# Image lines from two queues, fewer TensorE instructions ahead of the last one, pooled sums on VectorE: a start-up change to a fused attention and feed-forward kernel

**Chip, cores, metric.** One core of one Trainium2 chip. The metric is device time in microseconds (us), the median of several executions; a profile is one such execution. All times "at" a point are us from the start of the profiled span.

## The reference, cut to what matters

Four images are pooled 4x4, projected, and used as both keys and values of an attention with 12288 queries per image; the 49152 results go through a gated feed-forward layer.

```python
kv_pool = kv.reshape(B, H // r, r, W // r, r, C).mean(axis=(2, 4))      # r = 4, C = 128
k = v = kv_pool.reshape(B, -1, C) @ w_sr                                 # 768 keys per image
a = softmax(q @ k.transpose(0, 2, 1) / sqrt(C))
x = (a @ v).reshape(B * N, C)                                            # 49152 x 128
out = (relu(x @ w_gate) * (x @ w_val)) @ w_out                           # d_ff = 1536
```

## The kernel before

Queries are handled in tiles of 512. A loop over tiles `k` has twelve steps; in each, TensorE does one score, value, feed-forward and output matmul or so, of four different tiles. Before the loop, the first image has to be loaded, pooled, transposed and projected, and the first four tiles need scores. The 768 keys come as three pairs of 128-key chunks; each pair is loaded as four "lines" of 512 KB (rows `dh` of the 4x4 pooling). A "bank" in the code is a piece of the memory that takes TensorE's results; an "accumulator" is a bank that is held while several matmuls add into it. A load "lands" when its last byte has arrived.

```python
def kv_load(b, pair):                       # four loads of 512 KB on SyncE's queue
    ...
    for dh in range(r):
        nc.sync.dma_start(parts[:, dh]..., rows[dh])

def turn_add(chunk, lines, first=False):    # pool by transposing matmuls, summed in a bank
    if first: kv_Ts[chunk] = bank([128, 128])
    for i in range(lines.shape[1]):
        nc.tensor.matmul(kv_Ts[chunk], lines[:, i], ident, is_transpose=True, ...)

def values(k, jc, half):                    # two matmuls of 129 columns
    if jc == 0: x_banks[k, half] = bank([128, 2, C + 1])   # held until the last jc
    ...
# ---- first pair: four lines through TensorE as they land
for dh in range(3):
    for h in range(2): turn_add(h, line(0, dh, h), first=dh == 0)
...  # last line, projection, queries, eight scores
# ---- second pair: lines 0+1 added on VectorE, line 2, the sum and line 3 through TensorE
s1 = add_pixels(add_lines(1)); attend(0, 0)
...
for h in range(2):
    for half in range(2): values(1, h, half)       # first values of tiles 1 and 2
    project_chunk(2 + h, nc.scalar)
scores(0, 2); values(2, 0, 0); scores(0, 3); ...
attend(0, 1)
# ---- weights and the next queries on GpSimd's queue, gated behind line 2 of the third pair
nc.gpsimd.tensor_copy(gate, line(2, 2)[:, 0, 0, 0:1])
...  # wv, wg (halves), queries of group 1
q_turn(1)                                          # a transposing load, SBUF to SBUF: qT
nc.gpsimd.dma_start(wo16, ...)
# ---- last image line, then the loop
```

The transposing load `qT` gives the queries of tiles 4 to 7.

The softmax here doesn't subtract the row's maximum and nothing guards it: scores larger than these inputs give would overflow.

Of the kernel before, what the change touches and what calls it, by code (L numbers as in the profile page):

```python
# [10 lines left out]
FP16 = mybir.dt.float16  # L11
AF = mybir.ActivationFunctionType
ALU = mybir.AluOpType
# [3 lines left out]
def kernel(  # L17
# [23 lines left out]
    nc = tc.nc  # L41
# [5 lines left out]
    NJC = J // 128  # L47
# [7 lines left out]
    GRP = 4  # L55
# [8 lines left out]
    const = ctx.enter_context(tc.tile_pool(name="const", bufs=1))  # L64
# [4 lines left out]
    def bank(shape, dtype=FP32):  # L69
        return psum.tile(shape, dtype, tag="bank", name="bank_ps")  # L70
# [53 lines left out]
    def qT_of(k):  # L124
        s0 = (k % GRP) * NS
        return qTs[k // GRP][:, s0 : s0 + NS, :].rearrange("c s p -> c (s p)")
# [3 lines left out]
    kv16 = const.tile([128, B, NJC, 2 * C + 16], FP16)  # L130
    kv_in = {}

    def kv_load(b, pair):
        parts = work.tile([128, r, 2, r, C], FP32, tag="kv_in", bufs=3)
        rows = kv[b, pair * 2 * HC : (pair + 1) * 2 * HC].rearrange(
            "(hp dh) (wp h dw) c -> dh hp wp (h dw c)", dh=r, h=2, dw=r
        )
        for dh in range(r):
            nc.sync.dma_start(parts[:, dh].rearrange("p h dw c -> p (h dw c)"), rows[dh])  # L139
        kv_in[b, pair] = parts  # L140

    s3s, kv_Ts, key_banks = {}, {}, {}
# [15 lines left out]
    def turn_add(chunk, lines, first=False):  # L158

        if first:  # L160
            kv_Ts[chunk] = bank([128, 128])
        for i in range(lines.shape[1]):
            nc.tensor.matmul(  # L163
                kv_Ts[chunk], lines[:, i], ident, is_transpose=True,
                start=first and i == 0, stop=False, skip_group_check=True,
            )

    def turn_end(chunk, lines, engine=nc.vector):
        turn_add(chunk, lines)
        if chunk % 2 == 0:  # L170
            kv_Ts["pair"] = work.tile([128, 2, 128], FP32, tag="kvT", bufs=2, name="kvT")
        kvT = kv_Ts["pair"][:, chunk % 2]
        if engine is nc.scalar:
            nc.scalar.copy(kvT, kv_Ts[chunk])
        else:
            nc.vector.tensor_copy(kvT, kv_Ts[chunk])
        kv_Ts[chunk] = kvT

    def project_chunk(jc, engine=nc.vector):
        pr = bank([128, 128])  # L180
        nc.tensor.matmul(pr, w_sr_f32, kv_Ts.pop(jc), start=True, stop=True)  # L181
        if engine is nc.scalar:
            nc.scalar.mul(kv16[:, 0, jc, 0:C], pr, 1.0 / (r * r))  # L183
        else:
            nc.vector.tensor_scalar(kv16[:, 0, jc, 0:C], pr, 1.0 / (r * r), None, op0=ALU.mult)
# [9 lines left out]
    def turn_values(b, pair):  # L195
        vt = bank([128, 2, 128], FP16)
        for h in range(2):
            nc.tensor.transpose(vt[:, h], kv16[:, b, 2 * pair + h, 0:C], ident16)
        nc.vector.tensor_copy(kv16[:, b, 2 * pair : 2 * pair + 2, C : 2 * C], vt)
# [26 lines left out]
    def scores(k, jc):  # L226
        if jc == 0:
            aTs[k] = work.tile([128, NJC, T], FP16, tag="aT", bufs=4, name="aT")
        s_ps = bank([128, T])
        nc.tensor.matmul(s_ps, kv16[:, k // NST, jc, 0:C], qT_of(k), start=True, stop=True)  # L230
        nc.scalar.activation(aTs[k][:, jc, :], s_ps, AF.Exp, scale=qk_scale)  # L231

    def values(k, jc, half):
        if jc == 0:
            x_banks[k, half] = bank([128, 2, C + 1])
            if half == 0:
                x16s[k] = work.tile([128, NS, C], FP16, tag="x16", bufs=3, name="x16")
        x_ps = x_banks[k, half]
        for i in range(2):
            s = 2 * half + i  # L240
            nc.tensor.matmul(  # L241
                x_ps[:, i, :], aTs[k][:, jc, s * 128 : (s + 1) * 128],
                kv16[:, k // NST, jc, C : 2 * C + 1],
                start=(jc == 0 and i == 0), stop=(jc == NJC - 1), skip_group_check=True,
            )
# [150 lines left out]
    ident = const.tile([128, 128], FP32)  # L396
    make_identity(nc, ident)
    ident16 = const.tile([128, 128], FP16)
# [1 line left out]
    nc.gpsimd.memset(kv16[:, :, :, 2 * C : 2 * C + 16], 1.0 / X_SCALE)  # L400

    w_sr_f32 = const.tile([128, C], FP32)
    nc.scalar.dma_start(w_sr_f32, w_sr)
    kv_load(0, 0)
    for i in range(0, GRP, 2):
        q_load_plain(i, i + 2)
    for pair in range(1, NJC // 2):
        kv_load(0, pair)

    filler = const.tile([128, 512], FP16)  # L410
    nc.vector.memset(filler, 1.0)
    warm = const.tile([128, 1], FP32)
    nc.vector.memset(warm, 0.0)
    nc.scalar.activation(warm, warm, AF.Exp)
# [6 lines left out]
    idle = bank([128, 512])  # L421

    def fill(n):
        for _ in range(n):
            nc.tensor.matmul(idle, ident16, filler, start=True, stop=True)

    fill(8)

    def attend(k, pair):
        for jc in (2 * pair, 2 * pair + 1):  # L430
            for half in range(2):
                values(k, jc, half)

    def line(pair, dh, h=slice(0, 2)):
        return kv_in[0, pair][:, dh, h]

    def add_lines(pair):
        s2 = work.tile([128, 2, r, C], FP32, tag="kv_s2", bufs=2, name="kv_s2")
        nc.vector.tensor_tensor(s2, line(pair, 0), line(pair, 1), op=ALU.add)
        return s2  # L440

    def add_pixels(s2):
        s1 = work.tile([128, r, C], FP32, tag="kv_s1", bufs=2, name="kv_s1")
        s1 = s1.rearrange("p (h i) c -> p h i c", h=2)
        nc.vector.tensor_tensor(s1, s2[:, :, 0:2], s2[:, :, 2:4], op=ALU.add)
        return s1

    def scores_of(k, pair):
        for jc in (2 * pair, 2 * pair + 1):
            scores(k, jc)  # L450

    for dh in range(3):
        for h in range(2):
            turn_add(h, line(0, dh, h), first=dh == 0)
    for h in range(2):
        turn_end(h, line(0, 3, h), (nc.vector, nc.scalar)[h])
    for h in range(2):
# [11 lines left out]
    scores_of(2, 0)  # L469
    scores_of(3, 0)  # L470

    s1 = add_pixels(add_lines(1))
    attend(0, 0)
    for h in range(2):
        turn_add(2 + h, line(1, 2, h), first=True)
    for h in range(2):
        turn_add(2 + h, s1[:, h])
    for h in range(2):
        turn_end(2 + h, line(1, 3, h), nc.scalar)
    for h in range(2):  # L480
        for half in range(2):
            values(1, h, half)
        project_chunk(2 + h, nc.scalar)
    s2 = add_lines(2)
    scores(0, 2)
    values(2, 0, 0)
    scores(0, 3)
    scores(1, 2)
    scores(1, 3)
    values(2, 1, 0)  # L490
    scores_of(2, 1)
    nc.vector.tensor_tensor(s2[:, 0], s2[:, 0], line(2, 2)[:, 0], op=ALU.add)
    turn_values(0, 1)
    s1 = add_pixels(s2)
    turn_add(5, line(2, 2, 1), first=True)
    attend(0, 1)

    gate = const.tile([128, 1], FP32)
    nc.gpsimd.tensor_copy(gate, line(2, 2)[:, 0, 0, 0:1])
# [6 lines left out]

    for h in range(2):
        turn_add(4 + h, line(2, 3, h), first=h == 0)
    for h in range(2):
        turn_end(4 + h, s1[:, h], (nc.vector, nc.scalar)[h])  # L510
    scores(3, 2)
    for h in range(2):
        for half in range(2):
            values(1, 2 + h, half)
        project_chunk(4 + h, (nc.vector, nc.scalar)[h])
    scores_of(0, 2)
    turn_values(0, 2)
    for jc in (2, 3):
        values(2, jc, 0)
    scores_of(1, 2)  # L520
    attend(0, 2)
    for half in range(2):
        keep_sums(0, half)
# [6 lines left out]
    for jc in range(NJC - 2):  # L530
        values(2, jc, 1)
    late = [(2, 5), (3, 4), (3, 5)]
    left = {2: [(2, jc, half) for half in range(2) for jc in range(NJC - 2, NJC)]}
    for step, k, half in ((4, 3, 0), (7, 3, 1)):
        left[step] = [(k, jc, half) for jc in range(NJC // 2)]
        left[step + 1] = [(k, jc, half) for jc in range(NJC // 2, NJC)]
# [5 lines left out]
    for k in range(LAG, last + 1):  # L542
# [4 lines left out]
        b = k // NST + 1  # L547
        at = k % NST - (NST - NJC - 6)
        for step in range(NFB):
            kO, kF = k - LAG - 1, k - LAG  # L550
            half, i = divmod(step // 2, NJC // 2)
# [47 lines left out]
            if b < B:  # L599
                if step == 1 and 0 <= at < NJC and at % 2 == 0:  # L600
                    kv_load(b, at // 2)
                if step == 3 and 0 <= at - 2 < NJC:
                    pool_pixels(nc.gpsimd, b, (at - 2) // 2, at % 2)
                pair, odd = divmod(at - 4, 2)
                if 0 <= pair < NJC // 2:
                    if not odd and step == 1:
                        moves = turn_blocks(b, pair)
                    if moves and step > 4:
                        nc.sync.dma_start(*moves.pop())
                    if odd and step == 10:  # L610
                        project(b, pair)
                pair, odd = divmod(at - 6, 2)
                if 0 <= pair < NJC // 2 and not odd and step == 1:
                    turn_values_dma(b, pair)
# [33 lines left out]
```

## Time and profile before

| | before |
|---|---|
| median of runs (first five) | 1033.91 us (1033.40 to 1034.15) |
| profiled execution | 1033.09 us, span 1031.3 |
| TensorE busy | 99% |
| last image line lands | 23.09 |
| first instruction fetch of TensorE | 20.95, for 1.09 us |
| first feed-forward matmul ("loop start") | 30.30 |
| first output matmul (second pass) | 38.40 |

From about 34 us on TensorE is never idle for long, so a microsecond won ahead of that can be worth a microsecond at the end. And the profiled execution is one of the fastest of this kernel (1033.09 against a median of 1033.91), so totals of single profiles can't be compared at this scale; the times at which things happen inside them can.

### The profile page before, as it was taken

To read this page: it belongs to the slowest core of one execution; us is meant where nothing else is said; L and a number is where in the kernel's file an instruction comes from. 1 tells how busy PE (TensorE), PEld (TensorE's weight loads), DVE (VectorE), ACT (ScalarE), POOL (GpSimd) and SP (SyncE) were. 2 spreads that over 40 slices of the span, in tenths; PEclk is the share of its full clock that TensorE was granted. 3 is DMA by queue.
4 is the path that set the end of the run, shared out by engine and by line. 5 is a ranking of instruction groups with operands and counts; after the bars stand their busy time and mean duration, and the time that the engine had idled before them with its cause. 6 is when DMAs were issued, how large, how long until landed. Compare 5 with 4: busy or idle time off the path is not lost.

```text
span 1031.3 us, 20032 instructions
## 1 busy us (share of the span) xinstructions
PE 1024.4 (99%) x6580; PEld 546.0 (53%) x6580; DVE 910.0 (88%) x1671; ACT 908.8 (88%) x1745; POOL 279.4 (27%) x287
## 2 busy tenths in 40 slices
PE   8999999999999999999999999999999999999998
PEld 6555555555555555555555555555555555555555
DVE  3889899998989898998889898989888898989898
ACT  4988888889888889888888898888888988888987
POOL 2212146521211125642212121664121221111110
PEclk9999999999999999999999999999999999999999
DMA  8836396462542547836345157573652434513222
GB/s 305 122 57 76 90 195 144 79 93 42 82 69 48 80 120 162 169 53 90 52 68 86 33 84 151 131 173 57 85 73 46 73 54 65 87 32 65 34 40 54
DMA packets 328824, 93.34 MB, mean 91 GB/s; under 512 B 308496, under 2 KB 321936, under 8 KB 328720
## 3 DMA queue, kind: packets, MB, share of 16 engines
q1 hardware_dynamic: 313488, 78.69, 38.7%
q0 software_dynamic: 14944, 13.24, 10.9%
q8 instruction: 51, 0.84, 0.4%
q14 instruction: 53, 0.43, 0.1%
q10 hardware_dynamic: 288, 0.13, 0.0%
HBM read 53.94 MB, written 26.35 MB: 78 GB/s over the span
## 4 chain that ended last, share of the span: by engine, by line
PE 98%; ACT 1%; DMA 1%; SPq 0%; DVE 0%; issue 0%; ACTq 0%
PE bank_ps L279 24%; PE bank_ps L290 24%; PE bank_ps L314 23%; PE bank_ps L241 13%; PE bank_ps L230 12%; PE bank_ps L300 1%; DMA parts<-in_kv_dram 1%; PE bank_ps L163 1%; ACT aT L231 0%; PE bank_ps L189 0%; PE bank_ps L181 0%; SPq L139 0%; ACT val L283 0%; ACT kv L183 0%; PE bank_ps L119 0%
## 5 line engine op out<-in xcount | busy, mean ns | idle before, releaser
L293 DVE SCALAR_TENSOR_TENSOR hT<-bank_ps,val 128x512 f16<-128x512 f32 x1152 | 757.9, 686 | 91.1 <-ACT val L283 70.5
L283 ACT CAST val<-bank_ps 128x512 f16<-128x512 f32 x1152 | 677.8, 589 | 102.5 <-PE bank_ps L279 100.5
L279 PE MATMUL bank_ps<-xT,wv 128*128 128x512 f16 x1152 | 436.6, 379 | 0.2 <-DVE rinv L249 0.2
L290 PE MATMUL bank_ps<-xT,wg 128*128 128x512 f16 x1152 | 436.6, 379 | 0.0
L314 PE MATMUL bank_ps<-hT,wo 128*128 128x512 f16 x1116 | 423.0, 379 | 0.0
L231 ACT ACTIVATE aT<-bank_ps 128x512 f16<-128x512 f32 x576 | 345.8, 604 | 1.0 <-PE bank_ps L230 1.0
L324 POOL TENSOR_SCALAR o_sb<-o_t 128x512 f32<-128x512 f32 x93 | 138.3, 1487 | 694.1 <-DVE rinv L249 660.0
L241 PEld LDWEIGHTS <-aT 128*128 128x128 f16 x2304 | 177.3, 98 | 133.1 <-issue 0.9
L241 PE MATMUL bank_ps<-kv,aT 128*128 128x129 f16 x2304 | 223.6, 220 | 0.0
L230 PE MATMUL bank_ps<-qT,kv 128*128 128x512 f16 x576 | 217.3, 379 | 0.4 <-DVE qT L122 0.2
L279 PEld LDWEIGHTS <-wv 128*128 128x128 f16 x1152 | 112.7, 98 | 132.7 <-issue 0.3
L290 PEld LDWEIGHTS <-wg 128*128 128x128 f16 x1152 | 112.7, 98 | 67.3
L314 PEld LDWEIGHTS <-wo 128*128 128x128 f16 x1116 | 109.2, 98 | 65.9 <-issue 0.2
L230 PEld LDWEIGHTS <-kv 128*128 128x128 f16 x576 | 56.1, 98 | 67.6 <-issue 0.8
L257 DVE TENSOR_TENSOR x<-bank_ps,rinv 128x256 f16<-128x256 f32 x190 | 80.6, 424 | 6.6
L322 DVE STREAM_TRANSPOSE o_t<-bank_ps 128x512 f32<-128x512 f32 x93 | 65.7, 706 | 0.0
L86 POOL DMA_DIRECT2D q<-in_q_dram x88 | 48.3, 556 | 0.3 <-issue 0.3
L148 POOL TENSOR_TENSOR s<-parts 128x512 f32<-128x512 f32 x36 | 44.8, 1265 | 0.0
L249 DVE RECIPROCAL rinv<-bank_ps 128x2 f32<-128x2 f32 x192 | 27.9, 146 | 0.8 <-PE bank_ps L241 0.8
L150 POOL TENSOR_TENSOR s<-s 128x512 f32<-128x512 f32 x18 | 22.8, 1266 | 1.4
L152 POOL TENSOR_TENSOR c<-s 128x256 f32<-128x256 f32 x18 | 13.0, 724 | 1.4
L300 PEld LDWEIGHTS <-hT 128*128 128x128 f16 x144 | 10.1, 98 | 5.8
(53 smaller groups left out, 94.6 us busy)
## 6 DMA issues: line engine op xcount, KB each, us to landing
parts<-in_kv_dram SPq DMA_DIRECT2D x48, 512.0 KB, 6.5
out_dram<-o_sb SPq DMA_DIRECT2D x353, 64.0 KB, 2.2
q<-in_q_dram POOLq DMA_DIRECT2D x88, 128.0 KB, 4.6
xT<-x SPq DMA_TRANSPOSE x94, 2.4
out_dram<-o_sb SPq DMA_DIRECT2D x80, 16.0 KB, 1.5
placed<-blocks SPq DMA_DIRECT2D x9, 128.0 KB, 1.8
kvT<-placed SPq DMA_DIRECT2D x36, 32.0 KB, 1.9
q<-in_q_dram SPq DMA_DIRECT2D x2, 512.0 KB, 8.0
```

The costliest lines, as they stand in the source:

```text
L86: nc.gpsimd.dma_start(q16[32 * j : 32 * (j + 1)].rearrange("t (i s) c -> t i s c", i=GRP), rows[j])
L230: nc.tensor.matmul(s_ps, kv16[:, k // NST, jc, 0:C], qT_of(k), start=True, stop=True)
L231: nc.scalar.activation(aTs[k][:, jc, :], s_ps, AF.Exp, scale=qk_scale)
L241: nc.tensor.matmul(x_ps[:, i, :], aTs[k][:, jc, s * 128 : (s + 1) * 128], kv16[:, k // NST, jc, C : 2 * C + 1], start=(jc == 0 and i == 0) ...
L257: nc.vector.tensor_tensor(x16s[k][:, 2 * half : 2 * half + 2, :], x_ps[:, :, 0:C], rinv.to_broadcast([128, 2, C]), op=ALU.mult,)
L279: nc.tensor.matmul(va_ps, wv16[:, fb * 128 : (fb + 1) * 128], xTs[k], start=True, stop=True)
L283: nc.scalar.copy(val, va_ps)
L290: nc.tensor.matmul(g_ps, wg16[:, fb * 128 : (fb + 1) * 128], xTs[k], start=True, stop=True)
L293: nc.vector.scalar_tensor_tensor(hTs[k][:, fb, :], g_ps, 0.0, vals.pop((k, fb)), op0=ALU.max, op1=ALU.mult)
L314: nc.tensor.matmul(o_banks[k], wo16[:, fb, :], hTs[k][:, fb, :], start=fb == 0, stop=fb == NFB - 1)
L322: nc.vector.transpose(o_t, o_banks.pop(k))
L324: nc.gpsimd.tensor_scalar(o_sb.rearrange("t j s c -> t s j c"), o_t.rearrange("t (s j c) -> t s j c", s=NS, j=4), 1.0 / X_SCALE**2, None, ...
```

## The change

Intent: load the first four lines from two issuing engines; keep TensorE's instruction count ahead of the last image line low enough that the fetch of its next instructions doesn't share the DMA engines with that line; for that, add lines on VectorE and move twelve first value matmuls behind the line. (The prediction and the text below speak of "the title's 192": the title under which the change was handed over named that figure for the instruction count.)

```diff
-    def kv_load(b, pair):
+    def kv_load(b, pair, queues=(nc.sync,)):
...
-            nc.sync.dma_start(parts[:, dh]..., rows[dh])
+            queues[dh % len(queues)].dma_start(parts[:, dh]..., rows[dh])
...
-    nc.scalar.dma_start(w_sr_f32, w_sr)
-    kv_load(0, 0)
+    kv_load(0, 0, (nc.sync, nc.scalar))
+    nc.sync.dma_start(w_sr_f32, w_sr)
...
-            nc.tensor.matmul(idle, ident16, filler, start=True, stop=True)
-    fill(8)
+            nc.tensor.matmul(idle, ident, ident[:, 0:1].to_broadcast([128, 512]), ...)
+    fill(4)
...
-    for dh in range(3):
-        for h in range(2):
-            turn_add(h, line(0, dh, h), first=dh == 0)
+    s1 = add_pixels(add_lines(0))
+    for h in range(2): turn_add(h, line(0, 2, h), first=True)
+    for h in range(2): turn_add(h, s1[:, h])
...
-    s1 = add_pixels(add_lines(1))
+    s2 = add_lines(1)
+    for h in halves: add_third(1, s2, h)          # line 2 added on VectorE too
+    s1 = add_pixels(s2, halves)
     attend(0, 0)
...
-    for h in range(2):
-        for half in range(2): values(1, h, half)
         project_chunk(2 + h, nc.scalar)
...
-    scores(0, 2); values(2, 0, 0); scores(0, 3); scores(1, 2); scores(1, 3); values(2, 1, 0)
-    scores_of(2, 1)
+    for k in range(GRP - 1): scores_of(k, 1)
...
-    attend(0, 1)                                  # ahead of the last line
+    attend(0, 1)                                  # behind it, as are values(1, 0..1)
+    left[1] = [(2, jc, 0) for jc in range(NJC - 2)]   # tile 2's first values: in the loop
```

(Cut, and some lines joined; the loads of the weights and everything in the loop but `left` are unchanged.)

## The prediction

> **What bounds the kernel now.** I read the page first, then the chain of waits, then the timeline, the DMA view and busy time by windows for the first 40 us, because the diff touches nothing later than the first pass of the main loop. The page:
>
> ```profile
> span 1031.3 us, 20032 instructions
> PE 1024.4 (99%) x6580; PEld 546.0 (53%) x6580; DVE 910.0 (88%) x1671; ACT 908.8 (88%) x1745; POOL 279.4 (27%) x287
> ...
> PE 98%; ACT 1%; DMA 1%; SPq 0%; DVE 0%; issue 0%; ACTq 0%
> ```
>
> TensorE is busy for 99% of the span and is 98% of the chain that ended last. From about 34 us on, the chain is TensorE alone. So the change can only alter when the loop starts and how much TensorE work is then left over. The start reads as follows in the chain of waits:
>
> ```profile
> 2.75 7.00 DMA parts<-in_kv_dram
> ...
> 19.81 0.28 ACT kv L183
> 20.09 2.56 ACT aT L231 x5
> 22.64 0.04 issue
> 22.69 0.66 PE bank_ps L163 x4
> 23.34 0.45 PE bank_ps L241 x8
> 23.80 1.32 PE bank_ps L163 x12
> ...
> 29.73 0.42 DVE xT L274
> ...
> 30.30 0.39 PE bank_ps L279
> ```
>
> Columns: start, length, what. The reader should see that at 22.69 us TensorE begins the sums of the third pair of image chunks (L163), having waited for five exponentials of ScalarE, and that the first matmul of the feed-forward part (L279) comes at 30.30 us. From there to the end nothing in the order changes except eight small matmuls.
>
> The trace's landings of the single loads (14 of 512 KB) are 1.27 to 1.29 us apart from the fourth on; the last three image lines land at 19.98, 21.27 and 23.09. The last gap is 1.82. The DMA view of 20.75 to 21.00 us shows why:
>
> ```profile
> q1 hardware_dynamic: 20, 0.05, 50.3%
> q8 instruction: 1, 0.02, 27.3%
> ```
>
> One 16 KB packet of instructions took 27.3% of 16 engines' 0.25 us, so 1.09 us of one DMA engine. The sixteen completions of the last line show it: with the spacing of the line before, the last two were due at 22.02 and 22.55; they came at 22.51 and 23.09. So the fetch held the second-slowest engine back by 1.07 and the line by **0.54 us**. About 239 TensorE records (weight loads and matmuls) had started by then.
>
> **What the Trainium skill says.** (1) "Runtime: NRT & Kernel Launch", Instruction fetch mechanics: instructions come in blocks of 16 KiB, 256 instructions, over a DMA queue of the sequencer. The trace agrees: 51 packets and 0.84 MB on q8, and 215 to 302 TensorE records between the first fetches. (2) "TensorE: Matmul & The Clock Gate", Architectural detail: TensorE's queue is 64 deep. I read the title's 192 as 256 - 64; the trace has the fetch at 239, which doesn't contradict it, but doesn't show 192. (3) "DMA: Bandwidth & Descriptors", Issuing engines are not separate DMA queues: a second issuing engine saves only the issue time. Here a line takes 0.53 to 0.78 us to issue and 1.28 to move, so only the ramp can gain. (4) "PSUM — Partial Sum Buffer", Specifications: 8 banks. The trace agrees through the wait at 22.69: five accumulators of first values are held there, and L163, which needs a bank, waits for an exponential that frees one.
>
> **Part by part.**
>
> *First lines on two queues.* The bulk of the load is bound by transfer, 512 KB in 1.28 us, about 410 GB/s, and isn't shortened. The DMA view of 2 to 4 us has 0.40 MB, against 0.82 in each 2 us later: in 1.8 us from the first packet 0.74 MB were possible, so at most 0.34 MB or 0.82 us can be won. The first packets take 0.5 to 0.95 us each instead of 0.159, and a second queue only puts more of them in flight. I take half: **0.4 us**. The price: lines 0 and 1 share the engines, as do 2 and 3, so lines 2 and 3 should land together, at about 9.75 - 0.4 = 9.35. With the fetch gone too, the last line lands at 22.55 - 0.4 = **22.15** instead of 23.09.
>
> *Fewer instructions ahead.* Counting records (weight load plus matmul, twice that for plain fp32, as L181 shows) from the new order: fillers 16, transposing sums 40, projections 8, queries 32, scores 16, values' transposes 4, first values 16, then second pair 24, projections 8, scores 12, transposes 4, line 2 of the third pair 8: 188. Before, the same count is 268. The fetch moves behind the last line. It then falls among the weight loads, which aren't awaited.
>
> *Sums on VectorE.* 32 + 20 transposing matmuls of the first two pairs become 20 + 12. At 0.109 us each (12 in 1.32) this is 20 x 0.109 = 2.2 us less TensorE work, but in stretches where it waits for lines: from 5.23 to 22.69 us I count 5.6 us of idle time. VectorE gets, in the first pair, a 1.22 and a 0.69 us addition before line 3 lands, and in the second two more of some 0.69.
>
> It also delays keys. First pair: before, 8 transposes followed the last landing (9.75). Now lines 2 and 3 and the sum, 20, follow 9.35: the first half's sixteenth begins at 9.4 + 15 x 0.109 = 11.0 against 10.1, so the keys come 0.9 later. VectorE then reaches the second pair's additions at 15.24 + 0.9 = 16.15 and needs 1.22 + 2 x 0.69 + 0.4 until the first half is ready, 19.1; before, the sum was ready at 17.18. Two transposes, copy, projection and scaling as before (18.37 to 19.64) put the first score of that pair at about 20.6 instead of 19.64, and six scores of 0.216, the value transposes (0.11) and four sums (0.43) end near **22.45**. That is 0.3 behind the landing, and it sets the start.
>
> *First values behind the line.* Eight matmuls of tile 1 and four of tile 2, and four of line 2's transposes the other way. Only two accumulators are held before the last line instead of five, so the six scores don't wait for banks: VectorE's chain takes that wait's place at some 0.25 us less.
>
> *Work behind the last line until the loop.* With the trace's spacings (0.2155 for 512 columns, 0.0565 for a value matmul, 0.109 for fp32, 0.054 for an fp16 transpose):
> - Before, from 22.69 to the end of the first tile's values at 28.25 (5.56 us): 16 fp32 sums 1.74, 28 values 1.58, four records of projection 0.43, five scores 1.08, two transposes 0.11: 4.94, so 0.62 idle, mostly where a score waits for the scaled key of the sixth chunk (26.37 to 26.71).
> - After, from 22.45: 12 sums 1.31, 32 values 1.81, projections 0.43, five scores 1.08, transposes 0.11: 4.74. The order has values between projection and score, so I leave 0.3 idle: 27.5, **0.75 earlier**.
> - The rest to 30.30 is unchanged: it is VectorE's chain of reciprocals, scaling, transposing and copy, 2.05 us.
>
> *In the first pass.* Tile 2's first eight values now come in its second step: 0.45 us of TensorE. From 30.30 to 33.81 the chain alternates between ScalarE copies and exponentials (3.10 of 3.51 us busy), and TensorE's work is about 3.1, so some 0.4 is free for them: cost **0.1**.
>
> *Fillers.* Four fp32 of twice two passes last longer than eight fp16 but start some 0.4 earlier, without the memset, and warm the clock sooner (before, one took 0.43 cold). They end before 9 us, ahead of the first needed sum.
>
> Sum: 0.75 - 0.1 = 0.65; the pieces I rounded against the change (keys' delay, idle) could each be 0.2 to 0.3 smaller, so I predict a gain of **0.8 us**: 1033.91 - 0.8 = **1033.1 us**.
>
> **Rivals.** (a) *The landing sets the start*: TensorE is free when the last line lands and the sums begin at 22.15. For it: lines may land pairwise but line 2 first, and VectorE's additions may shift less. Then the gain is 0.75 + 0.3 - 0.1 = 0.95 or, with a ramp that gains the full 0.8 us, near 1.3: 1032.6 to 1033.0. (b) *VectorE takes the path*: the keys come later still, the first pair by over 1 us, the exponentials (0.51 us each in a row, six of them) end after 24 us, and the copy of the sixth chunk, behind them in ScalarE's order, is late. For it: VectorE has 4.1 us of additions where it had 1.9. Against it: in the run before it idled 2.89 us ahead of the third pair's first addition. Gain 0 to 0.3: 1033.6 to 1033.9. (c) *The work comes back*: twelve values moved behind the line (0.68 us) are paid in full because the first pass has no free time. Against it is the ScalarE-bound stretch. It takes 0.35 more: 1033.4. (d) *Fetch not avoided*, because it is triggered by another count: costs the 0.54 only if the landing sets the start.
>
> **Range and chances.** The rivals span 1032.6 to 1033.9, and the three runs before differ by 0.1. Range for 8 in 10: **1032.4 to 1033.8**. All of it is within 0.15% of before; 2% would be 20.7 us, more than the part of the span that is changed could give and far beyond any of the waits. Chances: faster 0.005, within 2% 0.99, slower 0.005.
>
> **What the new profile should show.** Right: lines 2 and 3 of the first pair landing together near 9.3; the q8 packet behind the last line's landing; that landing near 22.15; second pair's additions until about 19.1 on VectorE; scores of the second pair without a wait for a bank; last sums from 22.2 to 22.5; L279 near 29.55; 34 us onwards as before, shifted. Wrong: the q8 packet still ahead of the last landing; a wait of L163 for ScalarE or VectorE beyond 22.7; idle TensorE between 23 and 28 of over 0.6; or a loop that starts earlier while the end doesn't move.

## The result

| | before | after |
|---|---|---|
| median of five runs | 1033.91 (1033.40 to 1034.15) | 1033.38 (1032.09 to 1033.51) |
| ratio of fast runs | | 0.9992, 95% interval 0.9977 to 1.0006 |
| last image line lands | 23.09 | 21.86 |
| first fetch | 20.95 | 24.44 |
| loop start | 30.30 | 29.31 |
| first output matmul | 38.40 | 37.62 |
| second output matmul | 39.42 | **39.70** |

A ratio is the mean time of one kernel's fast runs over that of the other's of the same rounds, so not quite the ratio of the medians quoted. It is 0.9992, a gain of about 0.85 us in the mean and 0.53 in the median.

In the changed kernel's profile the lines have other numbers: L165 are the transposing sums (L163 before), L232 the scores (L230), L200 the values' transposes (L198), L281 and L292 the feed-forward matmuls (L279 and L290).

The table's last two rows are the surprise. The first output matmul is 0.78 us earlier than before and the second one 0.28 later. The page of the changed kernel has the trace of it in the chain that ended last, which had no transfer after the image lines before:

```profile
span 1031.6 us, 20001 instructions
PE 1022.9 (99%) x6560; PEld 543.9 (53%) x6560; DVE 913.4 (89%) x1676; ACT 909.5 (88%) x1745; POOL 279.9 (27%) x287
...
PE 96%; DMA 3%; POOL 0%; SPq 0%; ACTq 0%; issue 0%; ACT 0%
```

The chain of waits of the changed kernel from 20 to 41 us (start, length, what):

```profile
20.66 0.18 POOL gate L502
...
24.73 7.67 DMA q<-in_q_dram
...
32.56 6.66 DMA qT<-q
39.21 0.05 issue
39.26 0.39 PE bank_ps L232
```

and the waits of TensorE between 16 and 60 us (who waited for what: us in total, times, longest):

```profile
PE bank_ps L232 <- DMA qT<-q: 1.0, 1, 1.0
PE bank_ps L165 <- DVE kv_s L448: 0.7, 1, 0.7
```

The reader should see that up to 39.26 us the end hangs no longer on TensorE's own work but on the line that opens the gate, the queries' load behind it, and their transposing load. That load took 6.66 us from issue to landing; before it took 4.36 (33.06 to 37.42), 1.5 us ahead of its need at 38.93, by tile 4's scores in step 0 of the loop's second pass. Now it came 1.0 late. (The 0.7 us wait for VectorE, at 18.66, is taken up at the end of this section.)

What stretched it? The DMA view of the changed kernel, 35 to 36 us (queue: packets, MB, share of 16 engines):

```profile
q1 hardware_dynamic: 816, 0.21, 260.4%
q8 instruction: 1, 0.02, 6.8%
```

and 36 to 37 us:

```profile
q1 hardware_dynamic: 34, 0.01, 12.9%
```

The same microsecond, 36 to 37, of the kernel before, whose second fetch was over at 34.3:

```profile
q1 hardware_dynamic: 740, 0.18, 96.3%
```

In the changed kernel TensorE's second instruction fetch (one 16 KB packet) begins at 35.50 and takes 1.09 us, and from half a microsecond after its beginning the transposing load as a whole nearly stops for a microsecond. Before, that fetch lay at 33.43, ahead of the load's data. The change moved it: fewer instructions ahead mean that the count is reached later. The loads ahead can't be the reason: here they landed earlier than before (the queries at 32.40 against 32.90, `wo` at 34.75 against 35.27), and `qT` landed 1.79 later.

The start itself went as intended. TensorE in the changed kernel, 18 to 24 us (start, length, line, operation, count):

```profile
18.66 0.77 PE L165 MATMUL bank_ps<-ident,kv_s 128*128 128x128 f32 x4 [0.69 <-DVE kv_s L448]
...
20.31 1.59 PE L232 MATMUL bank_ps<-qT,kv 128*128 128x512 f16 x6
21.74 0.28 PE L200 MATMUL bank_ps<-ident,kv 128*128 128x128 f16 x2
21.88 1.15 PE L165 MATMUL bank_ps<-ident,parts 128*128 128x128 f32 x8
```

The six scores follow each other without a wait for a bank. The sums begin at 21.88, but the first four are of an earlier line; those of the last line, which landed at 21.86, begin at about 22.3 (21.88 and four sums of 0.109). So TensorE doesn't wait for the landing. What it waited for is VectorE's additions, at 18.66; from there on it has hardly a pause. The chain of the changed kernel with later scores (an experiment below, in which the wait for `qT` is gone) has these additions in it between 15.6 and 23 us, and no transfer:

```profile
16.85 1.29 DVE kv_s L480 x2
18.14 0.35 DVE kv_s L448
18.48 0.04 issue
18.53 0.78 PE bank_ps L165 x4
```

In the kernel before, TensorE came to the sums of the last line later, after its wait for a bank (22.69) and eight values:

```profile
23.63 1.04 PE L163 MATMUL bank_ps<-ident,parts 128*128 128x128 f32 x8
```

In that profile the line, landed at 23.09 with its fetch, had been there for half a microsecond: the fetch cost nothing there, and the bank set the start.

### The profile page after: what moved, and what is told of

Same layout as the page of the kernel before. It is cut to its first block, busy times and chain, and to the rows that moved or that the text cites. A ratio compares the mean times of both kernels' runs of the same rounds, so it can differ in the third digit from the quotient of the medians.

```text
span 1031.6 us, 20001 instructions
## 1 busy us (share of the span) xinstructions
PE 1022.9 (99%) x6560; PEld 543.9 (53%) x6560; DVE 913.4 (89%) x1676; ACT 909.5 (88%) x1745; POOL 279.9 (27%) x287
## 4 chain that ended last, share of the span: by engine, by line
PE 96%; DMA 3%; POOL 0%; SPq 0%; ACTq 0%; issue 0%; ACT 0%
PE bank_ps L292 24%; PE bank_ps L281 24%; PE bank_ps L316 23%; PE bank_ps L243 12%; PE bank_ps L232 12%; DMA parts<-in_kv_dram 2%; PE bank_ps L302 1%; DMA q<-in_q_dram 1%; DMA qT<-q 1%; PE bank_ps L191 0%; SPq L139 0%; POOL q L86 0%; POOL wv L504 0%; POOL wg L505 0%; ACTq L139 0%
## 5 line engine op out<-in xcount | busy, mean ns | idle before, releaser
L281 PE MATMUL bank_ps<-xT,wv 128*128 128x512 f16 x1152 | 436.6, 379 | 0.1
L292 PE MATMUL bank_ps<-xT,wg 128*128 128x512 f16 x1152 | 436.6, 379 | 0.0
L232 PE MATMUL bank_ps<-qT,kv 128*128 128x512 f16 x576 | 216.7, 379 | 1.2 <-DMA qT<-q 1.0
L281 PEld LDWEIGHTS <-wv 128*128 128x128 f16 x1152 | 112.7, 98 | 132.3
L292 PEld LDWEIGHTS <-wg 128*128 128x128 f16 x1152 | 112.7, 98 | 67.0
L232 PEld LDWEIGHTS <-kv 128*128 128x128 f16 x576 | 56.1, 98 | 69.2 <-DMA qT<-q 1.5
```

The lines of the kernel that those rows point to most:

```text
L232: nc.tensor.matmul(s_ps, kv16[:, k // NST, jc, 0:C], qT_of(k), start=True, stop=True)
L281: nc.tensor.matmul(va_ps, wv16[:, fb * 128 : (fb + 1) * 128], xTs[k], start=True, stop=True)
L292: nc.tensor.matmul(g_ps, wg16[:, fb * 128 : (fb + 1) * 128], xTs[k], start=True, stop=True)
```

## The experiments

Theory: the start gains about 1 us or more, through a last line that lands earlier and isn't held up by the fetch; a new collision, of the second fetch with the transposing load of `qT`, then takes a varying part of it. Rivals: `qT` is late because of the loads ahead of it alone; the gain is lost elsewhere; VectorE's sums or the values' new place, not the fetch, made the start faster. Kernels sent together ran on one chip and shared the runs of the kernel before (median 1033.76, 1033.86, 1033.18 and 1033.56 us in the four groups).

### The changed kernel again

> The changed kernel once more, unedited, because its five runs scattered from 1032.09 to 1033.51. Theory A (a collision): the second instruction fetch, which the lower count of TensorE instructions moved from 33.4 to 35.5 us, falls into the transposing load of qT and stretches it from 4.4 to 6.7 us, so TensorE waits some 1 us at 38 us for it; whether it collides fully differs between executions. Expected: runs again between 1032.0 and 1033.6, in a profile either a fetch near 35.5 and qT landing near 39.2, or an earlier landing and a span about 1 us shorter. Theory B (qT is late for another reason, the load of wo and of the queries ahead of it): qT lands at 39.2 in every execution, and the scatter comes from elsewhere.

No edit. Five runs from 1032.19 to 1033.27, median 1032.92, ratio 0.9992 again. In its profile (1032.92) the fetch is at 34.92, `qT` lands at 38.71, and the wait is 0.68 us. So the wait isn't the same in every execution, as theory A had it; it wasn't gone in this one.

### Taking the need for qT away

Later scores for tile 4:

```diff
+            elif k == GRP:
+                if step in (3, 5, 7, 9, 10, 11):
+                    scores(k, (3, 5, 7, 9, 10, 11).index(step))
             elif step % 2 == 0:
```

> The changed kernel with the six score matmuls of the fifth tile moved from steps 0, 2, 4, 6, 8, 10 of their pass to 3, 5, 7, 9, 10, 11: needed about 2.4 us later, so qT may land at 39.2 without a wait. Theory A and B: no wait for qT, total about 1032.2, and its runs scatter less than 0.4. If the gain of the start never reached the end for another reason (theory C: the time is given back later, in the tail or in the steady loop), the total stays near 1033.3 although the wait is gone.

Runs 1032.03 to 1032.33, median **1032.27**, ratio 0.9986 (0.9973 to 0.9998). In the profile `qT` lands at 37.97, TensorE's waits between 16 and 60 us are one line:

```profile
PE bank_ps L165 <- DVE kv_s L448: 0.7, 1, 0.7
```

The other line of the changed kernel is gone, and so, in these five runs, is the scatter. Against the changed kernel on the same chip (1032.92) that is 0.65 us less: so much of the gain in the median was lost in the wait, and theory C (lost later) falls.

The same again, on another chip:

> The changed kernel with later scores once more, unedited, on whichever chip comes, because it is the best version of the study and its margin of 0.7 us over the changed kernel is near the scatter of single runs. Expected: runs between 1031.9 and 1032.5, a ratio to the kernel before of 0.9985 to 0.9990; in the profile the first fetch behind the last line, the loop's first matmul near 29.2 and no wait for qT, whenever it lands. If in one of the runs the first fetch slips ahead of the last line, as it did with 28 records more, that run takes about 1033.

Ratio 0.9986 again (0.9972 to 1.0000), median 1032.21; but two of five runs were 1032.76 and 1032.95, outside what I expected. The profile is of the slowest. `qT` landed at 39.22 in it, as late as in the changed kernel, and wasn't waited for. It lost time at another place, which the timeline shows:

```profile
183.60 0.39 PE L281 MATMUL bank_ps<-xT,wv 128*128 128x512 f16 x1 [0.54 <-DMA xT<-x]
```

There a transposing load of `xT` was late in the loop. An instruction fetch began at 179.61, while it was under way; that this was the cause isn't tested (the count below, under the table, makes it likely).

The queries ahead of the second weight halves:

```diff
         nc.gpsimd.dma_start(wg16[:, own], moe_w_gate[:, own])
-    q_load(1)
+        if own.start == 0:
+            q_load(1)
     q_turn(1)
```

> The changed kernel with the second group's queries loaded ahead of the second halves of the feed-forward weights. Both theories: queries land near 30, the transposing load near 35, the wait for qT at 38 is gone, and the time falls to about 1032.2 (gain of 1.1 over the changed kernel's slower runs). If the second half of the weights then lands after 32.8, TensorE waits for it instead and the gain shrinks by that.

Median 1032.26 (1032.15 to 1032.88), ratio 0.9987: the wait is gone by another way. The path was not the expected one: the transposing load was issued at 30.31, two microseconds earlier, but landed at 37.69, not near 35, because it shared the engines with the weights until `wo` landed at 34.25, and because the second fetch (35.48) fell into it too. It was 0.36 us ahead of its need at 38.05.

The same later scores on the kernel before, as a control:

> The kernel before with only the later scores of the fifth tile (steps 3, 5, 7, 9, 10, 11), a control. If the wait for qT is a cost of the change alone, nothing changes: 1033.8, and the changed kernel with later scores (1032.27) keeps its 1.5 us over it. If the kernel before loses to the same collision in its usual executions (its profile, at 1033.09, was one of its fastest, and showed none), it falls to about 1033.1 with less scatter, and the change's own gain is then some 0.9 us.

1033.85 against 1033.86, ratio 1.0002 (0.9989 to 1.0014). The kernel before doesn't wait for `qT`; the wait is the change's own, and the change without it is worth some 1.4 us (0.9986, interval 0.9973 to 0.9998).

### Moving the fetches

28 more TensorE records (a record is one weight load or matmul in the trace), in idle time ahead of the first sums:

```diff
     fill(4)
+    for _ in range(14):
+        nc.tensor.matmul(idle[:, 0:128], ident16, ident16, start=True, stop=True)
```

> The changed kernel with 14 small fp16 matmuls (28 TensorE records, some 0.8 us) after its fillers, in time in which TensorE waits for lines anyhow. In the profiles so far the transposing load of qT landed 1.9 to 2.3 us after the load of wo when the second instruction fetch was at 34.13 or earlier or behind it, 2.6 with the fetch at 34.74, and 3.4 to 4.5 with a fetch from 34.9 to 35.5. Theory A (the fetch stretches the transposing load): 28 records move the fetch from about 35.5 to near 34.0, qT lands about 2.1 us after wo, near 37.0, the wait at 38 us is gone; the first fetch, near 22.9, stays behind the last line; total 1032.2 to 1032.4, as with later scores. Theory B (qT waits for wo and for the engines alone): qT lands at 38.5 or later still, total about 1033.

Half right, and not the clean test of theory A that it was meant to be. The second fetch moved to 33.20, `qT` landed at 37.54, and the wait for it was gone. But the load had moved too: it was issued at 31.98 and its first packet came at 33.27, so the fetch lay inside its data here as well, and it took 5.56 us. It was in time because it was issued 0.58 us earlier than in the changed kernel and took 1.10 less, and because TensorE needed it later (38.93). And the first fetch, which I had put at 22.9, behind the last line, came at 20.51, and the line landed 2.43 us after the one before it instead of 1.25: at 23.12. TensorE stood and waited:

```profile
21.99 0.65 PE L165 MATMUL bank_ps<-ident,parts 128*128 128x128 f32 x4
23.26 0.63 PE L165 MATMUL bank_ps<-ident,parts 128*128 128x128 f32 x4 [0.61 <-DMA parts<-in_kv_dram]
```

Loop start 30.17, total 1033.13, ratio 0.9998: 28 records undid the whole change in the median. They take it from 188 records ahead of the last line to 216, across the 192 of the title.

40 tiny matmuls for one filler, 76 records more:

```diff
-    fill(4)
+    fill(3)
+    for _ in range(40):
+        nc.tensor.matmul(idle[:, 0:32], ident16, ident16[:, 0:32], start=True, stop=True)
```

> 40 tiny matmuls (32 columns) take the place of one filler, in the idle time before the first needed sum: 76 more TensorE records ahead of the last line and of everything later, and nothing else. Theory A: the second fetch moves forward by the time of 76 records, to about 31.4 us, before the transposing load begins, so qT lands near 37.0 (4.4 us after its issue) and the wait of about 1 us for it is gone. At the same time the first fetch goes ahead of the last line, to about 19 to 20 us, and that line lands 0.35 to 1.07 us later than 21.86, which starts the loop up to 0.9 us later. Total 1032.4 to 1033.1. Theory B: qT still lands after 39, the loop starts later as well, total 1033.4 to 1034.

The first fetch came at 19.79 and the last line 2.21 us after the one before it, at 22.88, as expected. But the profile (1033.88) isn't a clean test of the loop start (31.01), because the clock fell. Busy time by windows (length, then PE, PEld, DVE, ACT, POOL busy, PEclk, DMA share, GB/s):

```profile
5.60:9.00 3.40, 1.68 (x42) 1.15 (x40) 1.92 (x2) 0.00 (x0) 0.00 (x0) 1.00 1.03 411
9.00:12.40 3.40, 3.35 (x16) 3.35 (x17) 0.00 (x0) 0.00 (x0) 0.00 (x0) 0.50 1.03 411
12.40:16.00 3.60, 3.12 (x22) 1.83 (x20) 2.11 (x7) 1.49 (x4) 0.00 (x0) 1.00 1.03 411
```

TensorE was busy for half of the first window, and the granted clock was 0.50 for the whole next one, in which the first pair's sums ran. Why isn't shown: windows of 3.41 us with as little work kept the full clock in other profiles (1.49 us busy from 5.73 in the one with values ahead, 1.67 from 5.45 in the changed kernel's second). The second fetch was at 34.12, not at 31.4 as I expected, because everything came later; `qT` landed 2.1 after `wo`. Runs at two levels, 1032.9 and 1034.0. A better made version, with TensorE as busy as before:

```diff
-    fill(4)
+    for _ in range(48):
+        nc.tensor.matmul(idle[:, 0:192], ident16,
+                         ident16[:, 0:1].to_broadcast([128, 192]), start=True, stop=True)
```
(on the version with later scores)

> The changed kernel with later scores, and its 4 plain fp32 fillers replaced by 48 fp16 matmuls of 192 columns, about as long: 80 more TensorE records ahead of the last image line (268, as many as in the kernel before) and TensorE as busy as it was. The scores being late, qT isn't awaited. Theory: the first fetch goes ahead of the last line (near 19 to 20 us) and the line lands 0.35 to 1.07 us later than 21.75; loop start (first feed-forward matmul) 0.2 to 0.9 later than 29.17; total 1032.5 to 1033.2 against 1032.27. Rival: the fetch costs nothing at the end because TensorE has other work then: total 1032.3.

The first fetch came at 18.00. The line under way landed 2.42 us after its predecessor (20.62 after 18.20), and the two behind it kept the delay: the last line at 23.14 instead of 21.75. Loop start 30.18, later by 1.01, a little more than expected; median 1033.05 against 1032.27, each beside its own runs of before (ratios 0.9994 and 0.9986). So a fetch ahead of the last line costs about 0.8 us at the end (the two intervals overlap, so the size is uncertain; the loop start shows it more plainly), and the loop start speaks against the rival that TensorE has other work then.

### The other parts, each undone alone (all with later scores)

The first lines on one queue:

```diff
-    kv_load(0, 0, (nc.sync, nc.scalar))
-    nc.sync.dma_start(w_sr_f32, w_sr)
+    nc.scalar.dma_start(w_sr_f32, w_sr)
+    kv_load(0, 0)
```

> The changed kernel with later scores, its first lines on the one queue as before. Theory: the last line lands about 0.4 to 0.7 us later than 21.75 (22.2 to 22.5) and the loop starts as much later, total about 1032.7 to 1032.9. Rival: TensorE reaches the last line only at 21.9 anyhow and takes up half of it: total 1032.5.

The last line landed at 22.45, 0.70 later; the loop started at 29.50, 0.33 later. Median 1032.57 (1032.16 to 1034.04), ratio 0.9992 (0.9980 to 1.0005, too wide to tell 0.3 us). In the profile the rival is right: half of the landing's gain is taken up. TensorE comes to the sums of the last line at about 22.2 with two queues, after the line, and with one queue at 22.58, when it waits 0.36 us. (The trace puts that wait down to an exponential; the line landed 0.13 ahead of its end.)

Sums of the first two pairs back on TensorE:

```diff
-    s1 = add_pixels(add_lines(0))
-    ... (line 2, the sum)
+    for dh in range(3):
+        for h in range(2): turn_add(h, line(0, dh, h), first=dh == 0)
...
-    for h in halves: add_third(1, s2, h)
...
+    for h in range(2): turn_add(2 + h, line(1, 2, h), first=True)
```

> The changed kernel with later scores, and the sums of the first two pairs as in the kernel before: 40 transposing matmuls (20 fp32 and 20 weight loads, 228 records ahead of the last line) come back to TensorE, VectorE's additions of the first pair and the third lines of the second go. Theory: the sums on VectorE delay the keys by about 1 us and TensorE waits 0.7 us for them at 18.5, so without them TensorE is free when the last line lands and the loop starts 0.3 to 0.5 earlier than 29.17, total 1031.8 to 1032.0; the sums on VectorE then earned their place only by the lower count. Rival: the fetch, at about record 233, now comes ahead of the landing or with it and delays it by 0.4 to 1.1: loop start 29.2 to 29.8, total 1032.3 to 1032.9.

The rival happened: 40 records more, first fetch at 20.96, last line at 23.27, and

```profile
21.27 0.61 PE L165 MATMUL bank_ps<-ident,parts 128*128 128x128 f32 x4
23.40 0.63 PE L165 MATMUL bank_ps<-ident,parts 128*128 128x128 f32 x4 [1.52 <-DMA parts<-in_kv_dram]
```

TensorE is ready 0.5 us earlier than with the sums on VectorE (21.27 against 21.74) and then waits 1.52 for the line. Loop start 30.31. Of five runs three took 1033.12 to 1033.19 and two 1031.77 and 1032.05. The profile is of the slower kind. That the faster ones are executions in which the fetch missed the line fits the other runs, but they weren't traced. If it is so, sums on TensorE without the fetch are no slower than on VectorE, and VectorE earns its place by the lower count alone.

Twelve value matmuls ahead of the line again:

```diff
+        for half in range(2): values(1, h, half)
         project_chunk(2 + h, nc.scalar)
...
+    scores(0, 2); values(2, 0, 0); scores(0, 3); scores(1, 2); scores(1, 3); values(2, 1, 0)
...   (attend(0, 1) ahead of the last line, left[1] taken out)
```

> The changed kernel with later scores, and twelve first value matmuls (and the first tile's eight) put ahead of the last line again, as before: five accumulators are held, 228 records ahead of the line, so the fetch should stay behind it. Theory: TensorE waits for banks near 21.7 to 22.7 as in the kernel before (for exponentials that free one), so the last line's sums begin near 22.5 to 23, while twelve values less are left afterwards: loop start within 0.3 of 29.17, total within 0.3 of 1032.27. Rival: work ahead of the line is free, and the loop starts 0.5 earlier: 1031.8.

My expectation was wrong by 1.7 us in the median and 2.2 at the loop start: 31.36, median 1033.94, ratio 1.0005 (0.9992 to 1.0019). The line landed undelayed (22.21, 1.24 after its predecessor; in this execution all lines were some 0.46 later from the first one on). TensorE:

```profile
22.27 0.86 PE L232 MATMUL bank_ps<-qT,kv 128*128 128x512 f16 x2
23.25 0.27 PE L200 MATMUL bank_ps<-ident,kv 128*128 128x128 f16 x2
23.74 0.66 PE L165 MATMUL bank_ps<-ident,parts 128*128 128x128 f32 x4 [0.22 <-ACT aT L233]
```

Five accumulators are held again, so the bank for the third pair's next sums has to be freed by an exponential, as in the kernel before; but with VectorE's sums the keys, and so the exponentials, come later (first score of the pair at 20.69 against 19.64 there). The wait ends at 23.74 against 22.69 (0.46 of it is this execution's late lines). So sums on VectorE with values ahead gain nothing over the kernel before, while with the values behind the line they gain 1.4 us: the values had to go behind the line *because* the sums went to VectorE.

### The kernel before, a second profile

> The kernel before, unedited, for a second profile, because its first one (1033.09) was among its fastest and its median is 1033.8 to 1033.9. If its scatter comes from the first fetch (which engine it holds back), the last line lands later than 23.09 in a slower execution and the loop starts as much later than 30.30; if it comes from the second fetch, qT lands after 38.9 and TensorE waits for it; if from neither, the loop starts at 30.3 and the difference lies later.

1033.33 us in this one look; its state can't be told from one run. The chain of waits:

```profile
12.24 11.47 DMA parts<-in_kv_dram
23.71 0.14 issue
23.85 1.50 PE bank_ps L163 x12
```

The last line landed at 23.71, 0.62 later than in the first profile, with the fetch at 20.62. The chain now goes through the line, and the loop started at 30.54, 0.24 later; the span is 0.24 longer. TensorE came to the sums of the last line at 23.85 instead of 23.63: in this execution the fetch did cost something, in the first it didn't. So this part of the scatter is the first fetch's. The median executions near 1033.8 were not profiled, and what they lose beyond that stays open.

### The fetches in one table

From the traces of the runs. "Gap" is between the last line's landing and that of the line before (others: 1.25 to 1.29). "Records" is how many TensorE records had started at the first fetch, without the sequencer's own instructions (235 for the first profile of before; the prediction's 239 includes four of those).

| kernel | first fetch | records | gap of last line | loop start | second fetch | `qT` after `wo` | `qT`, issue to landing |
|---|---|---|---|---|---|---|---|
| before | 20.95 | 235 | 1.82 | 30.30 | 33.43 | 2.15 | 4.36 |
| before, again | 20.62 | 233 | 2.54 | 30.54 | 33.11 | 2.47 | 4.89 |
| before, later scores | 21.10 | 233 | 1.80 | 30.49 | 34.07 | 1.92 | 4.97 |
| sums on TensorE | 20.96 | 217 | 2.60 | 30.31 | 33.00 | 2.16 | 4.92 |
| 28 records more | 20.51 | 194 | 2.43 | 30.17 | 33.20 | 1.77 | **5.56** |
| 76 records more | 19.79 | 224 | 2.21 | 31.01 | 34.12 | 2.09 | 4.37 |
| 80 records more | 18.00 | 228 | 1.26 (an earlier line 2.42) | 30.18 | 34.13 | 1.98 | 4.95 |
| values ahead | 21.51 | 191 | 1.24 | 31.36 | 36.29 | 2.33 | 4.36 |
| one queue | 22.20 | 188 | 1.23 | 29.50 | 34.74 | 2.56 | **5.97** |
| after | 24.44 | 227 | 1.25 | 29.31 | 35.50 | 4.47 | **6.66** |
| after, again | 24.91 | 243 | 1.25 | 29.15 | 34.92 | 4.18 | **6.25** |
| later scores | 24.67 | 237 | 1.25 | 29.17 | 35.18 | 3.45 | **5.53** |
| later scores, again | 24.53 | 229 | 1.24 | 29.34 | 35.09 | 4.24 | **6.27** |
| queries first | 24.43 | 227 | 1.24 | 29.29 | 35.48 | 3.43 | **7.37** |

Two readings. First, the fetch cost the last line nothing where it began behind its landing or at most 0.74 us ahead of the time at which it was due (the landing before it plus 1.28: one queue, values ahead), and it cost a line 0.55 to 1.35 us (gap less 1.25) where it began 0.98 us or more ahead of that time. Second, `qT`. Its first packet comes about 1.3 us after its issue (1.65 with the queries first). Where the fetch was over at most 0.45 us after that packet, or began only in the load's last 0.6 us, the load took 4.36 to 4.97 us from issue to landing; where the fetch lay inside its data for 0.88 us or more (bold), 5.53 to 6.66, and 7.37 with the queries first. When the load begins is set by the loads ahead of it (theory B has that right); how long it takes goes with the fetch. The column "after `wo`" hides this in two rows, 28 records more and one queue, where `wo` itself was late (35.76 and 36.77).

The loop tests the same on other loads. In the fourteen kept traces, 817 transposing loads of `xT` had no other transposing load and no packet of GpSimd's queue beside them. The 684 without a fetch of TensorE's instructions took 2.44 us in the median, nine in ten of them at most 2.51; the 133 that a fetch overlapped took 3.27, and up to 4.59. Where the fetches lay among these loads was nobody's choice, so this supports theory A better than the single runs do; how a fetch stretches such a load stays open.

## Why the prediction was right, step by step

The time (1033.38 against 1033.1, inside the range) and the gain (predicted 0.8; 0.53 in the median, about 0.85 in the mean) were right. The number alone proves little: the ratio's interval (0.9977 to 1.0006) doesn't exclude no gain at all, and the five runs before differ by 0.75 us, not by the 0.1 of the three that the prediction had seen. The start was right in mechanism and somewhat too cautious, and one wait was missing.

| step | predicted | measured |
|---|---|---|
| first pair's lines 2 and 3 land | together, 9.35 | 8.93 and 8.62 |
| last line lands | 22.15 | 21.86 |
| fetch | behind it | 24.44 |
| first score of second pair | 20.6 | 20.31 |
| sums of the last line start | 22.45 | about 22.3 |
| loop start | 29.55 | 29.31 |
| given back in the first pass | 0.1 | 0.21 (8.10 before, 8.31 after) |
| later waits | none | 1.03 for `qT` |

- **Two queues.** I took half of a possible 0.82 us. One queue instead of two moved the landing by 0.70, so the ramp gains more than half. (My reading that the first packets take 0.5 to 0.95 us each was too dark: of the first forty, 19 took under 0.25.) At the loop it was worth 0.33 in the profiles.
- **Fetch.** I put the held-up line at 0.54 us, from one profile. Other executions without the change's low count had 0.55 to 1.35 (values ahead excepted, where it came late): the first profile was a mild one. That the removal would be worth having at the end was right: restoring the count cost 1.01 us at the loop start and about 0.8 at the end.
- **192.** I read it as 256 less a queue of 64 and noted that the trace's count of 235 didn't show it. Runs now lie near it at the low end: the earliest fetches begin with 188, 191 and 194 records started, and 216 records ahead of the line were too many where 188 were not. Others begin with up to 243, and what triggers a fetch isn't shown. My expectation for the 28 records more went wrong by trusting the count of 233 to 243 instead.
- **VectorE and banks.** No bank wait, and TensorE comes to the last line after its landing, by 0.45 us (I had 0.3), held up by VectorE's additions: the central case, not rival (a), is what happened. The keys were later by less than the 0.96 that I worked out: 0.67 (first score of the second pair at 20.31 against 19.64 before), with the first pair's lines landed by 8.93 and not at 9.35. In rival (b) I put VectorE's additions at 4.1 us; the terms that I named add up to about 5.2, which is what the trace has in the first two pairs (1.92 and 3.27). They fitted all the same.
- **First pass.** Twice what I took, 0.2 us: the eight values found less free time than the 0.4 I counted.
- **What failed.** "34 us onwards as before, shifted" did not hold. I had the fetch falling "among the weight loads, which aren't awaited", and looked no further than the first fetch: with fewer instructions ahead, every later fetch moves too, and the second went from 33.43 to 35.50, into a transposing load that had 1.5 us to spare before. That took 0.7 to 1.0 us of a gain of 1.0 to 1.4 in the two profiles. That the total came out near the prediction is luck: without the wait the gain is 1.45 us in the mean (1032.22 against 1033.67 on the same chip), 0.65 more than predicted, and the wait took back 0.65 (1032.87 in the mean). In the profiles the loop starts 0.24 to 0.40 earlier than predicted; the rest is likely that the kernel before usually runs slower than the profile that I worked from (1033.09).

What beat both kernels is the changed kernel with tile 4's scores up to three steps later: ratio 0.9986 to the kernel before on two chips (medians 1032.27 and 1032.21). With the changed kernel it was compared on one chip only.

## What to carry to other kernels

A one-packet instruction fetch can delay the awaited load that it falls into (here by 0.55 to 1.35 us for an image line), so at microsecond scale the instruction count is part of the schedule: know where the fetches lie, and after a change look at all of them, not at the one you moved. When a change brings the start of a long, full pipeline forward, list the loads whose slack it eats: here `qT`, with 1.5 us of slack, became the new wait when the start gained about 1 us and the load itself took 2.3 us more. And two parts of a change can each depend on the other: in these runs sums on VectorE paid only with values behind the line.

## What the Trainium skill lacked or had wrong

- "Runtime: NRT & Kernel Launch", Instruction fetch mechanics: says that crossing a block boundary is mostly hidden. Here the 16 KB packets took 0.88 to 1.67 us of one DMA engine in the traces' first two fetches, and delayed an awaited 512 KB load by 0.55 to 1.35 us where they began 0.98 us or more ahead of the time at which it was due; restoring such a fetch cost about 0.8 us at the end. It says that the next block is fetched while the current one runs, but not when: here with 188 to 243 TensorE records started.
- "DMA: Bandwidth & Descriptors", DMA Transpose (X-bar): nothing on what an instruction fetch does to a transposing load. Here one fetch of 1.09 us was followed by a near stop of the whole load (34 packets in a microsecond against 740); with a fetch inside its data `qT` took 5.53 to 7.37 us instead of 4.36 to 4.97, and the loop's `xT` loads 3.27 in the median instead of 2.44.
- The same page, Issuing engines are not separate DMA queues: says that a second issuing engine saves only the issue time, usually small. The kind agrees, the "small" doesn't at the head of a queue: here it brought the last of fourteen 512 KB loads 0.70 us forward in the profiles (an issue took 0.53 to 0.78 us, a transfer 1.28), and the loop 0.33.
- "TensorE: Matmul & The Clock Gate", What's actually happening: names an idle window as what lowers the clock, but no share of busy time at which that happens. Here the busy time of a window doesn't tell: 1.68 us of 3.40 was followed by a granted clock of 0.50 in one profile, while 1.49 and 1.67 of 3.41 in two others kept the full clock.
